# One set of PSUM pools in an attention and soft mixture-of-experts kernel, and another pace in its tail

## The chip, the cores and the metric

The kernel runs on one core of one Trainium2 chip. The time is device microseconds (us) of an execution; a comparison goes by the median of several runs. Engines are called TensorE (PE in the rows), VectorE (DVE), ScalarE (ACT), GpSimd (POOL) and SyncE (SP, whose queue issues all DMAs here). PSUM is the memory that TensorE writes, in 8 banks of 512 fp32 columns by 128 partitions.

## What is computed

Causal attention with a bias from a running sum, on 8 batches of 8 heads, 576 positions of 64 columns; its output, as 4608 tokens of 512 columns, goes through a soft mixture of 8 experts with 4 slots each.

```python
def reference(q, k, v, s, phi, w1, w2):                 # q, k, v (8, 8, 576, 64); s (8, 8, 576)
    scores = q @ k.T / 8                                # per batch and head
    cum = cumsum(maximum(s, 0), -1)
    scores = where(causal, -1e9, scores + minimum(-(cum[:, None] - cum[None, :]), 0))
    attn = exp(scores - max); attn /= attn.sum(-1) + 1e-9
    x = (attn @ v).reshape(4608, 512)                   # tokens
    logits = x @ phi                                    # (4608, 32)
    d = softmax(logits, over tokens); c = softmax(logits, over slots)
    slot_input = (d.T @ x).reshape(8, 4, 512)
    for e in range(8):                                  # w1 (8, 512, 1024), w2 (8, 1024, 512)
        slot_out[e] = maximum(slot_input[e] @ w1[e], 0) @ w2[e]
    return c @ slot_out.reshape(32, 512)                # (4608, 512)
```

## The kernel before

The attention part, up to about 376 us, is a list of operations, each with an engine, an estimated duration, what it comes after, and how many PSUM banks it takes. `schedule` (line 34) puts them in one order per engine; the program is then traced in that order by the loop at line 920. PSUM is divided there into a ring of six banks, `bank()` (line 169, pool `psm`), and two single banks `y` and `sum` (pool `psy`). Where the planner leaves TensorE a gap near the end, `busy(n)` (line 913) fills it with n products of no use. The last operations of the list make the softmax over the tokens final: `m0` to `m7` (lines 794 to 832) end with `i4s`, a scaled 128 x 32 matrix; `t8` (line 780) adds the last batch to `acc`, the sum of tokens by slots; and `ct`/`cd` (lines 706 to 720), per batch, transpose the tokens' weights of the slots and copy them to `ctw`, for the output.

Then `actx.close()` (line 931) releases the list's pools, and the tail follows in the order in which it is written:

- Lines 936 to 945: a new pool `ps4` of eight banks over all of PSUM, given out in turn by `bk()`. The slots' input `sit` is made by four products of `acc` and `i4s`, and copied by VectorE.
- `mlp1` (line 951), the first expert layer, for two groups of four experts: 4 steps of 8 products each with 512 columns, four of them side by side on strips of 32 columns of the array. After each step, `refill` (line 1036) has SyncE load the next four weight blocks of `w2` into the tiles of `w1` that the step was the last to read. `turn` (line 968) transposes the result, with VectorE's copy.
- `mlp2(half, eg)` (line 982), the second layer, for a half of the 512 columns and a group: 8 steps of 4 products of 256 columns. Both groups of a half write one bank, `pso[half]`, in its two halves; VectorE copies the first group's (256 columns), ScalarE the second's.
- `pick(half)` (line 995) sorts the slots by two products `sel`; ScalarE and VectorE make of them `sl[half]`, a high and a low part.
- `result(half, beside)` (line 1010) makes the output: 36 tiles of 128 tokens, two to a bank (`po`), copied by VectorE and ScalarE in turn, and written in nine DMAs of four tiles (512 KB). After every two banks, `result(0)` advances the second layer of half 1 by two steps (line 1029); what is left of it, and `pick(1)`, stand behind its last output. Then `result(1)` runs alone.

All weights are 64 blocks of 512 KB. The first 43 are loaded during the list, into tiles that it does not need or no longer needs; the other 21 are those of `refill`. Every DMA stands in SyncE's one queue, in the order of the text. On this chip an fp32 product is two rows of TensorE in the profile, so a step of `mlp1` is 16 rows and one of `mlp2` is 8.

Of the kernel before, what the change touches and what calls it, by code (L numbers as in the profile page):

```python
# [102 lines left out]
def tile_attn_softmoe(ctx: ExitStack, tc, qk, v, s, phi, w1, w2, cst, out):  # L103
# [9 lines left out]
    NS = 32  # L113
# [20 lines left out]
    tot = top.tile([128, 2], F32, name="tot")  # L134
    nc.vector.memset(tot, 0.0)
    one1 = top.tile([1, 1], F32, name="one1")
    nc.vector.memset(one1, 1.0)
    pre = top.tile([128, NPRE * F], F32, name="pre")

# [23 lines left out]
    one = actx.enter_context(tc.tile_pool(name="one", bufs=1))  # L163
    p2 = actx.enter_context(tc.tile_pool(name="p2", bufs=2))
    pd = actx.enter_context(tc.tile_pool(name="pd", bufs=3, space=bass.MemoryType.DRAM))
    psm = actx.enter_context(tc.tile_pool(name="psm", bufs=6, space=PSUM))
    psy = actx.enter_context(tc.tile_pool(name="psy", bufs=1, space=PSUM))

    def bank(name):
        return psm.tile([128, 512], F32, tag="bank", name=name)  # L170
# [68 lines left out]
    def op(key, eng, ns, prio, fn, after=(), bank=0, frees=None, dma=0, ldw=107, tail=107, mode=0):  # L239

        assert key not in ops, key
        t = prio[0]
        for x in prio[1:]:
            t += PR[x[0]][x[1]] if isinstance(x, tuple) else PR[x]
        ops[key] = dict(eng=eng, ns=ns, prio=round(t, 6), fn=fn, after=[a for a in after if a is not None], bank=bank,
                        frees=frees or [], dma=dma, pt=prio, ldw=ldw, tail=tail, mode=mode)
# [581 lines left out]
    def m7():  # L828
# [2 lines left out]
        nc.vector.reciprocal(t, t)  # L831
        nc.vector.tensor_scalar(i4s, i4, t, st["fac"][:, 1:2], op0=ALU.mult, op1=ALU.mult)

    def load_phi():
        nc.sync.dma_start(out=ph, in_=phi)

# [12 lines left out]
    for i, (e, ns, fn) in enumerate((("PE", 107, m0), ("DVE", 300, m1), ("PE", 60, m2), ("DVE", 100, m3), ("ACT", 220, m4),  # L849
                                     ("DVE", 100, m5), ("PE", 160, m6), ("DVE", 400, m7))):  # L850
        op(("m", i), e, ns, (8.0 * B - 400 + i * 0.1, "soft"), fn, [prev] + {5: [("t4", B - 1)], 6: [("cst",)]}.get(i, []), bank=int(e == "PE"),
           frees=[(("m", i - 1), 0)] if i in (1, 3, 7) else None)
        prev = ("m", i)
    op(("cst",), "SP", 450, (3.0,), (fetch, cst_sb, cst), [("load", 3)], dma=450)
    op(("cw",), "SP", 450, (2.5,), lambda: nc.sync.dma_start(out=cumd, in_=cumhl), [("cum", 1)], dma=800)
    op(("phi",), "SP", 650, (2.0,), load_phi, [("load", 2)], dma=728)
# [56 lines left out]
    def busy(n):  # L913
        d = psy.tile([128, 512], F32, tag="y", name="busy")
        for i in range(n):
            nc.tensor.matmul(d[:, 0:128], ident, ident, start=True, stop=True)
# [16 lines left out]

    tb = ctx.enter_context(tc.tile_pool(name="tb", bufs=1))
    to = ctx.enter_context(tc.tile_pool(name="to", bufs=1))
    ps4 = ctx.enter_context(tc.tile_pool(name="ps4", bufs=8, space=PSUM))

    def bk(name):
        return ps4.tile([128, 512], F32, tag="bk", name=name)

    ps = bk("sit")
    for cc in range(NCC):
        nc.tensor.matmul(ps[:, 32 * cc:32 * cc + 32], acc[:, 128 * cc:128 * cc + 128], i4s, start=True, stop=True)  # L943
    sit = tb.tile([128, NCC, NS], F32, name="sit")
    nc.vector.tensor_copy(sit, ps[:, 0:128].rearrange("p (c s) -> p c s", c=NCC))

    ht = tb.tile([128, 2, NFC, 128], F32, name="ht")

    hs = []

    def mlp1(eg):
        pss = [bk(f"m1{eg}{half}") for half in range(F // 512)]
        for cc in range(NCC):
            for half in range(F // 512):
                for g in range(4):
                    nc.tensor.matmul(pss[half][32 * g:32 * g + 32, :], sit[:, cc, :],  # L956
                                     w1q[4 * eg + g, cc][:, 512 * half:512 * half + 512],
                                     start=(cc == 0), stop=(cc == NCC - 1))
            yield
        relu(eg, pss)  # L960
# [6 lines left out]

    def turn(eg):
        for half in range(F // 512):
            pt = bk(f"ht{eg}{half}")  # L970
            for f in range(4):
                nc.tensor.transpose(pt[:, 128 * f:128 * f + 128],  # L972
                                    hs[eg][:, 512 * half + 128 * f:512 * half + 128 * f + 128], ident)
            nc.vector.tensor_copy(ht[:, eg, 4 * half:4 * half + 4, :], pt.rearrange("p (f x) -> p f x", f=4))
# [2 lines left out]
    cts = [ctw[i // 2][:, 2 * (i % 2):2 * (i % 2) + 2] for i in range((B + 1) // 2)]  # L977

    HC = DM // 2
    pso, sl = [], []  # L980

    def mlp2(half, eg):

        if eg == 0:
            pso.append(bk(f"m2{half}"))
        ps = pso[half][:, HC * eg:HC * eg + HC]
        for fc in range(NFC):
            for g in range(4):
                w = w2q[4 * eg + g, 2 * half + fc // 4]
                nc.tensor.matmul(ps[32 * g:32 * g + 32, :], ht[:, eg, fc, 32 * g:32 * g + 32],  # L990
                                 w[:, HC * (fc % 4):HC * (fc % 4) + HC], start=(fc == 0), stop=(fc == NFC - 1))
            yield
        (nc.scalar.copy if eg else nc.vector.tensor_copy)(sos[half][:, eg, :], ps)  # L993

    def pick(half):

        ps = bk(f"sel{half}")
        for eg in range(2):
            nc.tensor.matmul(ps[0:96, 0:HC], sel[eg], sos[half][:, eg, :], start=(eg == 0), stop=(eg == 1))  # L999
        t = sl[half]  # L1000
        nc.scalar.copy(t, ps[0:96, 0:HC])  # L1001
        nc.vector.tensor_tensor(t[64:96, :], ps[64:96, 0:HC], t[64:96, :].bitcast(F32), op=ALU.subtract)  # L1002
# [3 lines left out]
    def steps(it, n=100):  # L1006
        for _ in range(n):
            next(it, None)

    def result(half, beside=iter(())):  # L1010
        k = 0
        outc = out[:, HC * half:HC * half + HC].rearrange("(t p) c -> p t c", p=128)
        for i in range(0, NO, 4):
            m = min(4, NO - i)
            ot = stage.pop(0)[:, 0:m * HC].rearrange("p (t c) -> p t c", t=m)
            for j in range(0, m, 2):
                n = min(2, m - j)
                po = bk(f"po{half}_{i + j}")[:, 0:n * HC].rearrange("p (t c) -> p t c", t=n)
                for x in range(n):
                    b, c = divmod(i + j + x, 9)  # L1020
                    cv = cts[b].rearrange("p b s -> p (b s)")[:, 128 * c:128 * c + 128]
                    nc.tensor.matmul(po[:, x, :], cv, sl[half], start=True, stop=True)  # L1022
                if k % 2 == 0:
                    nc.vector.tensor_copy(ot[:, j:j + n, :], po)  # L1024
                else:
                    nc.scalar.copy(ot[:, j:j + n, :], po)  # L1026
                k += 1
                if k % 2 == 0:
                    steps(beside, 2)
            nc.sync.dma_start(out=outc[:, i:i + m, :], in_=ot)  # L1030

    again.sort(key=lambda x: x[0])
# [23 lines left out]
    steps(mlp2(0, 0))  # L1056
    steps(mlp2(0, 1))
    pick(0)
    m = chain(mlp2(1, 0), mlp2(1, 1))
    result(0, m)  # L1060
    steps(m)
    pick(1)
    result(1)


# [49 lines left out]
```

## Time and profile before

| | |
|---|---|
| time, median of 3 runs | 443.43 us (442.27 to 443.96) |
| span of the profiled execution | 445.1 us (the page gives no other time of it) |
| TensorE busy | 411.9 us, 93% of the span |
| VectorE, ScalarE, GpSimd busy | 307.0, 245.8, 281.5 us |
| moved by DMA | 83.21 MB, mean 187 GB/s |

The page cuts the span into 40 slices of 11.1 us. In all but the last six TensorE is busy for 0.89 or more of a slice and the DMA engines mostly for 0.3 to 0.7; in the last slices the DMA engines are at 0.8 to 0.99 and move 278 to 414 GB/s, the last two of them with TensorE busy 0.6 and 0. One slice near the tail has a granted TensorE clock of 0.6 to 0.7, where 1 is 2.4 GHz and 0.5 is 1.2 GHz. A profile is one execution; its span stands 1.7 us above the median.

### The profile page before, as it was taken

The page shows a single profiled execution, that of the slowest core. Times are in us where ns is not written, and L with a number is a line of the kernel's source. Part 1 is how long each engine was busy: PE and PEld are TensorE (multiplying, and loading weights), DVE is VectorE, ACT ScalarE, POOL GpSimd, SP SyncE. Part 2 cuts the span into 40 slices and gives each one's busy share as a digit, 9 for nine tenths or more (in the row PEclk, how much of TensorE's full clock was granted, in tenths as well). Part 3 has the DMA queues.
Part 4 walks back from the last instruction along what each step waited for, and adds up shares of the span by engine and source line. Part 5 has one row for each costly group of instructions (what it writes and reads, how often), then busy time and mean ns, then how long its engine had stood idle before and what let it go on. Part 6 is the DMA issues. An engine that isn't in the chain of part 4 may idle for free. (4 is left out here: it accounts for less than half of the span.)

```text
span 445.1 us, 14696 instructions
## 1 busy us (share of the span) xinstructions
PE 411.9 (93%) x5631; PEld 305.1 (69%) x5631; DVE 307.0 (69%) x1055; ACT 245.8 (55%) x732; POOL 281.5 (63%) x385
## 2 busy tenths in 40 slices
PE   8799999989999999999999999999999998998960
PEld 7687777777677767766877677777777766334550
DVE  6777767987887878778877987888685667021460
ACT  2236577576657665856665676576766735021350
POOL 6339989878876896888588868897888700000000
PEclk9699999999999999999999999999999999699995
DMA  5317556636664475447544832461356499899988
GB/s 173 107 46 216 172 161 173 191 107 184 178 194 130 135 207 162 130 134 221 162 127 136 221 87 83 119 185 57 109 135 187 118 300 404 278 414 406 356 279 294
DMA packets 54549, 83.21 MB, mean 187 GB/s; under 512 B 5456, under 2 KB 41808, under 8 KB 54480
## 3 DMA queue, kind: packets, MB, share of 16 engines
q1 hardware_dynamic: 54480, 82.29, 59.0%
q8 instruction: 44, 0.72, 0.7%
q14 instruction: 25, 0.20, 0.1%
HBM read 71.84 MB, written 10.06 MB: 184 GB/s over the span
## 5 line engine op out<-in xcount | busy, mean ns | idle before, releaser
L323 DVE CUSTOM_DVE_ANT_0 junk<-mx,mask 128x448 bf16<-128x448 f32 (+3 forms) x320 | 125.6, 427 | 52.5 <-PE mx L311 27.1
L388 ACT ACTIVATE arena<-s 128x288 f32<-128x288 f32 (+4 forms) x384 | 114.3, 406 | 30.1 <-PE s L377 29.4
L377 PE MATMUL s<-w 64*128 64x288 f32 (+4 forms) x1152 | 109.2, 304 | 0.0
L478 PE MATMUL y<-arena 128*64 128x512 f32 (+4 forms) x640 | 90.1, 427 | 0.0
L377 PEld LDWEIGHTS s<-w 64*128 64x128 f32 (+1 forms) x1152 | 81.9, 177 | 10.0 <-issue 1.2
L395 POOL TENSOR_SCALAR_AFFINE_SELECT arena<-arena 128x256 f32<-128x256 f32 (+1 forms) x160 | 68.1, 437 | 23.3 <-ACT arena L388 21.2
L478 PEld LDWEIGHTS y<-arena 128*64 128x64 f32 x640 | 43.0, 137 | 46.4 <-issue 35.8
L421 POOL TENSOR_TENSOR arena<-arena 128x896 f32<-128x896 f32 x31 | 66.9, 2159 | 7.9 <-PE mt L346 5.9
L311 PE MATMUL mx<-w 64*128 64x288 f32 (+4 forms) x384 | 58.8, 312 | 4.5 <-DVE e_nat L664 2.7
L377 PE MATMUL s<-g 64*128 64x288 f32 (+4 forms) x384 | 56.7, 291 | 0.0
L311 PE MATMUL mx<-g,ones 64*128 64x288 f32 (+4 forms) x384 | 55.1, 305 | 1.3 <-POOL g L217 1.3
L423 POOL TENSOR_TENSOR arena<-arena 128x640 f32<-128x640 f32 x31 | 48.0, 1548 | 2.6
L278 ACT CAST w<-arena 128x576 fp32r<-128x576 f32 x64 | 39.8, 676 | 16.1 <-DMA arena<-in_qk_dram 16.1
L283 DVE TENSOR_TENSOR w<-arena,w 128x576 fp32r<-128x576 f32 x64 | 47.8, 773 | 0.0
L311 PEld LDWEIGHTS mx<-w 64*128 64x128 f32 x384 | 40.6, 189 | 8.7 <-PE s L377 3.9
L490 ACT COPY arena<-y 128x512 f32<-128x512 f32 x32 | 18.8, 588 | 46.6 <-PE y L478 46.6
L311 PEld LDWEIGHTS mx<-g,ones 64*128 64x128 f32 x384 | 40.4, 190 | 2.0 <-POOL g L217 1.5
L540 DVE TENSOR_TENSOR arena<-arena 128x576 f32<-128x576 f32 x31 | 31.6, 1033 | 10.4 <-DMA arena<-rs 10.0
L377 PEld LDWEIGHTS s<-g 64*128 64x128 f32 (+1 forms) x384 | 35.3, 176 | 0.6 <-DMA g<-hl 0.2
L338 POOL TENSOR_SCALAR mh<-mx 128x10 fp32r<-128x10 f32 x32 | 21.1, 658 | 20.6 <-DVE mx L323 20.6
L425 POOL TENSOR_TENSOR arena<-arena 128x384 f32<-128x384 f32 x31 | 31.5, 1015 | 2.4
L323 DVE CUSTOM_DVE_ANT_0 junk<-mx,mask,mx 128x288 bf16<-128x288 f32 x64 | 30.6, 516 | 2.2 <-PE mx L311 1.2
(157 smaller groups left out, 577.0 us busy)
## 6 DMA issues: line engine op xcount, KB each, us to landing
pre<-in_w_dram SPq DMA_DIRECT2D x38, 512.0 KB
arena<-in_qk_dram SPq DMA_DIRECT2D x32, 576.0 KB
arena<-in_w_dram SPq DMA_DIRECT2D x18, 512.0 KB
arena<-rs SPq DMA_DIRECT2D x62, 144.0 KB
arena<-in_v_dram SPq DMA_DIRECT2D x32, 256.0 KB
out_dram<-arena SPq DMA_DIRECT2D x11, 512.0 KB
out_dram<-pre SPq DMA_DIRECT2D x7, 512.0 KB
wg<-in_w_dram SPq DMA_DIRECT2D x5, 512.0 KB
```

The costliest lines, as they stand in the source:

```text
L278: nc.scalar.copy(w[:, QO + S * i:QO + S * (i + 1)], st["raw", p][:, i, :])
L283: nc.vector.tensor_tensor(w[:, QO + S * (2 + i):QO + S * (3 + i)], st["raw", p][:, i, :], w[:, QO + S * i:QO + S * (i + 1)].bitcast(F32), ...
L311: nc.tensor.matmul(ps[a][:, d:d + hi - lo], l[r], t[r, KO + lo:KO + hi], start=t is w, stop=t is gt)
L323: nc.vector.tensor_tensor_reduce(out=junk[r, 0:w], in0=ps[r, d:d + w], in1=mask[r, o:o + w], scale=1.0, scalar=m[:, a, 4:5] if i == 1 else ...
L377: nc.tensor.matmul(ps[a][0:n, d:d + hi - lo], t[r, ko + 128 * j:ko + 128 * j + n], t[r, qo + lo:qo + hi], start=x == 0, stop=x == 3)
L388: nc.scalar.activation(st["p", p][0:n, a, o + lo:o + hi], ps[0:n, d:d + hi - lo], AF.Exp, bias=0.0, scale=0.125)
L395: nc.gpsimd.affine_select(d, d, pattern=[[0, 2], [1, n]], compare_op=ALU.is_ge, fill=0.0, base=0, channel_multiplier=-1)
L421: eng.tensor_tensor(z[:, :, 128:576], pt[:, :, 128:576], pt[:, :, 576:1024], op=ALU.add)
L423: eng.tensor_tensor(z[:, :, 256:576], z[:, :, 256:576], pt[:, :, 1024:1344], op=ALU.add)
L425: eng.tensor_tensor(z[:, :, 384:576], z[:, :, 384:576], pt[:, :, 1344:1536], op=ALU.add)
L478: nc.tensor.matmul(y[r, lo - 64:512], vt[:, j, r], st["p", p][:, g, OFF[j] + lo - 128 * j:OFF[j] + 576 - 128 * j], start=(j == 0), stop=(j ...
L540: nc.vector.tensor_tensor(u, u, st.pop(("r", p)), op=ALU.mult)
```

## The change

There are four edits, all in the tail or next to it.

1. The pools `psm` and `psy` live to the end, and `ps4` is gone: `bk()` becomes `bank()`, six banks in a ring.
2. The slots' input is made by two operations of the list, `sit0` (TensorE, behind three filler products) and `sit1` (VectorE's copy). The last batch's transposes `ct` come after `sit0`. The tile `sit` moves to a pool that lives throughout.
3. `mlp2` writes each group into a bank of its own, `y` and `sum`.
4. `result` takes a list of steps: behind its outputs of four tiles, 2, 3, 3, 3, 3, 3 and 1 steps of what stands beside it, which is the second layer of half 1 and, as its last step, `pick(1)`. The outputs 7 and 8 (counted from 0) have none.

```diff
-    psm = actx.enter_context(tc.tile_pool(name="psm", bufs=6, space=PSUM))
-    psy = actx.enter_context(tc.tile_pool(name="psy", bufs=1, space=PSUM))
+    psm = ctx.enter_context(tc.tile_pool(name="psm", bufs=6, space=PSUM))
+    psy = ctx.enter_context(tc.tile_pool(name="psy", bufs=1, space=PSUM))
...
+    def sit0():
+        busy(3)
+        st["sit"] = bank("sit")
+        for cc in range(NCC):
+            nc.tensor.matmul(st["sit"][:, 32 * cc:32 * cc + 32], acc[:, 128 * cc:128 * cc + 128], i4s, start=True, stop=True)
+
+    def sit1():
+        nc.vector.tensor_copy(sit, st.pop("sit")[:, 0:128].rearrange("p (c s) -> p c s", c=NCC))
...
+    op(("sit", 0), "PE", 900, (8.0 * B - 500, "soft"), sit0, [prev, ("t8", B - 1)], bank=1)
+    op(("sit", 1), "DVE", 290, (8.0 * B - 500, "soft"), sit1, [("sit", 0)], frees=[(("sit", 0), 0)])
+    ops["ct", B - 1]["after"].append(("sit", 0))
...
-    ps4 = ctx.enter_context(tc.tile_pool(name="ps4", bufs=8, space=PSUM))
...
-    ps = bk("sit")
-    for cc in range(NCC):
-        nc.tensor.matmul(ps[:, 32 * cc:32 * cc + 32], acc[:, 128 * cc:128 * cc + 128], i4s, start=True, stop=True)
-    sit = tb.tile([128, NCC, NS], F32, name="sit")
-    nc.vector.tensor_copy(sit, ps[:, 0:128].rearrange("p (c s) -> p c s", c=NCC))
...
-        if eg == 0:
-            pso.append(bk(f"m2{half}"))
-        ps = pso[half][:, HC * eg:HC * eg + HC]
+        ps = psy.tile([128, 512], F32, tag=("y", "sum")[eg], name=f"m2{half}{eg}")[:, 0:HC]
...
-    def result(half, beside=iter(())):
+    def result(half, beside=iter(()), pace=()):
...
-                if k % 2 == 0:
-                    steps(beside, 2)
+            if i // 4 < len(pace):
+                steps(beside, pace[i // 4])
             nc.sync.dma_start(out=outc[:, i:i + m, :], in_=ot)
...
-    m = chain(mlp2(1, 0), mlp2(1, 1))
-    result(0, m)
-    steps(m)
-    pick(1)
+    def rest():
+        yield from chain(mlp2(1, 0), mlp2(1, 1))
+        yield
+        pick(1)
+
+    result(0, rest(), (2, 3, 3, 3, 3, 3, 1))
     result(1)
```

Up to these places every engine has the same instructions in the same order; GpSimd and SyncE have them to the end. The rows below are the built programs' order, without times; a name is the tile written, then the tiles read, and the number in a name only keeps tiles apart.

TensorE at the end of the list, before: filler (`busy`), the last batch's transposes (`ctb`, `cta`), the slots' input (`sit`) and the first product of the first layer (`m`).

```order
L916 MATMUL busy<-ident 128x128 x4
L711 MATMUL ctb_7259<-ident,en_7231 96x128
L711 MATMUL cta_7258<-ident,en_7231 96x128 x4
L943 MATMUL sit<-i4s,acc 128x32 x4
L956 MATMUL m_7289<-pre,sit 32x512 x4
```

The same place now:

```order
L929 MATMUL busy<-ident 128x128 x4
L839 MATMUL sit<-i4s,acc 128x32 x4
L712 MATMUL ctb_7266<-ident,en_7232 96x128
L712 MATMUL cta_7265<-ident,en_7232 96x128 x4
L959 MATMUL m_7285<-pre,sit 32x512 x4
```

The slots' input has moved ahead of the last transposes; there are as many filler products.

TensorE at the first half of the second layer, before: the last transposes of the first layer's result (`ht`), then both groups' products, all on one bank.

```order
L972 MATMUL ht_7402<-ident,h_7393 128x128 x4
L990 MATMUL m_7410<-arena,ht 32x256 x35
L990 MATMUL m_7410<-pre,ht 32x256
L990 MATMUL m_7410<-arena,ht 32x256 x3
L990 MATMUL m_7410<-pre,ht 32x256
```

Now:

```order
L975 MATMUL ht_7398<-ident,h_7389 128x128 x4
L991 MATMUL m_7406<-arena,ht 32x256 x32
L991 MATMUL m_7440<-arena,ht 32x256 x3
L991 MATMUL m_7440<-pre,ht 32x256
L991 MATMUL m_7440<-arena,ht 32x256 x3
```

The products are the same; behind the 32 of the first group the tile written is another one.

TensorE at the end of `result(0)`, before: outputs (`po`, by the number of their first tile), the second layer's products of half 1 (`m`), the pick (`sel`) and the first output of half 1 (`po_0`).

```order
L1022 MATMUL po_24_7586<-sl_7408,ct_6978 128x256 x2
L1022 MATMUL po_26_7590<-sl_7408,ct_6978 128x256 x2
L990 MATMUL m_7490<-pre,ht 32x256 x8
L1022 MATMUL po_28_7603<-sl_7408,ct_6978 128x256 x2
L1022 MATMUL po_30_7607<-sl_7408,ct_6978 128x256 x2
L990 MATMUL m_7490<-pre,ht 32x256 x8
L1022 MATMUL po_32_7620<-sl_7408,ct_6978 128x256 x2
L1022 MATMUL po_34_7624<-sl_7408,ct_6978 128x256 x2
L999 MATMUL sel_7630<-pre,cst_sb 96x256 x2
L1022 MATMUL po_0_7635<-sl_7409,ct_6977 128x256 x2
```

Now:

```order
L1023 MATMUL po_20_7583<-sl_7404,ct_6979 128x256 x2
L1023 MATMUL po_22_7587<-sl_7404,ct_6979 128x256 x2
L991 MATMUL m_7548<-pre,ht 32x256 x8
L1023 MATMUL po_24_7601<-sl_7404,ct_6979 128x256 x2
L1023 MATMUL po_26_7605<-sl_7404,ct_6979 128x256 x2
L1000 MATMUL sel_7609<-pre,cst_sb 96x256 x2
L1023 MATMUL po_28_7615<-sl_7404,ct_6979 128x256 x2
L1023 MATMUL po_30_7619<-sl_7404,ct_6979 128x256 x2
L1023 MATMUL po_32_7624<-sl_7404,ct_6979 128x256 x2
L1023 MATMUL po_34_7628<-sl_7404,ct_6979 128x256 x2
L1023 MATMUL po_0_7633<-sl_7405,ct_6978 128x256 x2
```

The second layer's last products stand two outputs earlier, and the pick stands ahead of the last two outputs of half 0 instead of behind them.

## Rows read from the trace of the kernel before

**Rows 1.** Tail by stretches: length, each engine's busy us, clock, DMA share, GB/s.

```profile
376.00:383.00 7.00, 4.99 (x31) 2.88 (x33) 1.46 (x5) 0.69 (x2) 0.00 (x0) 0.74 1.01 402
...
383.00:386.00 3.00, 3.00 (x20) 0.81 (x16) 0.00 (x0) 0.00 (x0) 0.00 (x0) 0.50 0.32 81
386.00:390.00 4.00, 4.00 (x44) 1.28 (x40) 0.00 (x0) 0.17 (x1) 0.00 (x0) 0.98 0.94 294
390.00:410.00 20.00, 18.47 (x221) 8.26 (x213) 3.52 (x6) 2.96 (x6) 0.00 (x0) 1.00 1.03 412
...
420.00:428.00 8.00, 6.57 (x69) 3.78 (x62) 2.91 (x6) 2.83 (x6) 0.00 (x0) 1.00 0.88 300
428.00:430.00 2.00, 2.00 (x19) 2.00 (x19) 2.00 (x4) 1.87 (x4) 0.00 (x0) 1.00 0.16 57
430.00:443.50 13.50, 1.92 (x17) 1.72 (x15) 3.36 (x6) 2.63 (x6) 0.00 (x0) 0.65 1.02 340
```

**Rows 2.** The same view, two stretches, for the clock (third number from the end).

```profile
378.00:380.00 2.00, 1.22 (x9) 1.18 (x8) 0.00 (x0) 0.69 (x2) 0.00 (x0) 0.84 1.04 416
...
408.00:410.00 2.00, 1.09 (x5) 0.47 (x4) 0.42 (x1) 0.51 (x2) 0.00 (x0) 1.00 1.05 410
```

**Rows 3.** SyncE in order of time: start, length, what it issues, how many.

```profile
384.39 9.42 SPq L838 DMA_DIRECT2D pre<-in_w_dram  x12
...
411.16 7.04 SPq L1030 DMA_DIRECT2D out_dram<-arena  x5
```

**Rows 4.** TensorE's waits from 376 to 446, all: us, times, longest.

```profile
PE po L1022 <- DVE sl L1002: 1.8, 2, 0.9
PE m L990 <- DVE pre L993: 1.4, 2, 0.9
PE sit L943 <- ACT ct L720: 0.8, 1, 0.8
PE ctb L711 <- DVE en L704: 0.7, 1, 0.7
PE sel L999 <- ACT pre L993: 0.5, 1, 0.5
PE m L956 <- issue: 0.5, 1, 0.5
```

**Rows 5.** TensorE, then VectorE, in order of time at the end of the list.

```profile
375.51 1.06 PE L916 MATMUL busy<-ident 128*128 128x128 f32 x8
...
377.44 0.60 PE L711 MATMUL cta<-ident,en 128*96 128x128 f32 x4
378.82 1.47 PE L943 MATMUL sit<-i4s,acc 128*128 128x32 f32 x8 [0.78 <-ACT ct L720]
...
375.92 0.30 DVE L832 TENSOR_SCALAR i4s<-cst_sb,tot,fac 128x32 f32<-128x32 f32 x1
...
380.38 0.29 DVE L945 COPY sit<-sit 128x128 f32<-128x128 f32 x1 [3.21 <-PE sit L943]
```

**Rows 6.** The chain that ended last, in the tail: start, length, what, rows merged.

```profile
380.77 13.16 PE m L956 x96
...
394.96 3.62 PE m L956 x32
...
404.04 3.66 PE m L990 x64
...
409.78 0.74 PE po L1022 x4
410.51 1.00 PE m L990 x16
411.52 0.67 PE po L1022 x4
...
427.35 2.92 PE po L1022 x22
...
432.77 0.60 DVE pre L1024
```

More of the change, by code (lines that the diff above doesn't have):

```diff
@@ L136, in tile_attn_softmoe @@
     one1 = top.tile([1, 1], F32, name="one1")
+    sit = top.tile([128, DM // 128, NS], F32, name="sit")
     nc.vector.memset(one1, 1.0)
@@ L935, in tile_attn_softmoe @@
     to = ctx.enter_context(tc.tile_pool(name="to", bufs=1))
-    ps4 = ctx.enter_context(tc.tile_pool(name="ps4", bufs=8, space=PSUM))
-    def bk(name):
-        return ps4.tile([128, 512], F32, tag="bk", name=name)
-    ps = bk("sit")
-    for cc in range(NCC):
-        nc.tensor.matmul(ps[:, 32 * cc:32 * cc + 32], acc[:, 128 * cc:128 * cc + 128], i4s, start=True, stop=True)
-    sit = tb.tile([128, NCC, NS], F32, name="sit")
-    nc.vector.tensor_copy(sit, ps[:, 0:128].rearrange("p (c s) -> p c s", c=NCC))
     ht = tb.tile([128, 2, NFC, 128], F32, name="ht")
@@ L951, in mlp1 @@
     def mlp1(eg):
-        pss = [bk(f"m1{eg}{half}") for half in range(F // 512)]
+        pss = [bank(f"m1{eg}{half}") for half in range(F // 512)]
         for cc in range(NCC):
@@ L969, in turn @@
         for half in range(F // 512):
-            pt = bk(f"ht{eg}{half}")
+            pt = bank(f"ht{eg}{half}")
             for f in range(4):
@@ L979, in tile_attn_softmoe @@
     HC = DM // 2
-    pso, sl = [], []
+    sl = []
     def mlp2(half, eg):
-        if eg == 0:
-            pso.append(bk(f"m2{half}"))
-        ps = pso[half][:, HC * eg:HC * eg + HC]
+        ps = psy.tile([128, 512], F32, tag=("y", "sum")[eg], name=f"m2{half}{eg}")[:, 0:HC]
         for fc in range(NFC):
@@ L995, in pick @@
     def pick(half):
-        ps = bk(f"sel{half}")
+        ps = bank(f"sel{half}")
         for eg in range(2):
@@ L1017, in result @@
                 n = min(2, m - j)
-                po = bk(f"po{half}_{i + j}")[:, 0:n * HC].rearrange("p (t c) -> p t c", t=n)
+                po = bank(f"po{half}_{i + j}")[:, 0:n * HC].rearrange("p (t c) -> p t c", t=n)
                 for x in range(n):
```

## The prediction, made before the changed kernel was run

> **What bounds the kernel now.** I read the page first (the span, the slices, the chain), then the last 70 us by stretches [rows 1], then what SyncE issues [rows 3] and what TensorE waits for [rows 4], and last the chain through the tail [rows 6]. The order of instructions shows that up to 375 us each engine does what it did before, so only the tail can move the time. There the reader is to see two things.
>
> First, the DMA engines bound the tail, not TensorE. From 376 on they have to bring the last of the first 43 weight blocks, then 21 more into tiles that the first layer has finished with, and to write 18 outputs, 512 KB (0.524 MB) each. Their share is about full at 412 GB/s while they read and at 340 while they write [rows 1], and after TensorE's last product (it starts its last run of them at 427.35) they write for 13 us more [rows 1, 6]. The span ends 1.6 us behind the last write.
>
> Second, they run dry twice. From 383 to 390 they carry 81 and then 294 GB/s, because SyncE issues nothing until 384.39 [rows 1, 3]: the first block of the 21 goes into a tile that the first layer must have read. From 420 to 430 they carry 300 and then 57, because outputs come too slowly and then, around the second pick, not at all [rows 1]. What the change is worth is what it fills of these two holes; a TensorE that is early by more than that gains nothing.
>
> **The holes in us.** By bytes the first is (412 - 81) x 3 / 412 + (412 - 294) x 4 / 412 = 2.4 + 1.1 = 3.5; by the DMA share (1 - 0.32) x 3 + (1 - 0.94) x 4 = 2.3. The second is by bytes, against the 340 of pure writing, (340 - 300) x 8 / 340 + (340 - 57) x 2 / 340 = 0.9 + 1.7 = 2.6; by share 1.0 + 1.7 = 2.7. Together 5.0 to 6.1 us [rows 1]. That is the ceiling of the gain, whatever TensorE does: the same bytes are moved at the same rates.
>
> **Part 1: the input of the slots, made in the list.** Before, its products stood behind the last transposes and waited 0.8 us for ScalarE's copy of these, since the new pool takes over the banks of the old [rows 4]; they ran from 378.82 for 1.47 us, VectorE's copy and the hops took until 380.77 [rows 5, 6]. Now they stand ahead of the last transposes. Their input i4s is there at 375.92 + 0.30 = 376.2, TensorE's filler ends at 375.51 + 1.06 = 376.6 [rows 5] (there are four filler products as before: one from the list, three in the new step), so they run from 376.6 to at most 378.1. The transposes behind them took about 0.7 us (from 377.32, the first one, to 378.04 [rows 5]); the copy (0.29 [rows 5]) lies beside them. The first layer starts at 378.8 instead of 380.77: **2.0 us earlier**. The transposes end some 0.7 us later than before; their ScalarE copies feed only outputs 30 us on, so that costs nothing.
>
> The clock is the other half of it. The granted clock falls between 378 and 380, mean 0.84 (from 2.4 to 1.2 GHz), is 0.50 from 383 to 386 and back at 0.98 from 386 on [rows 1, 2], after TensorE had stood still 0.7 us for the transposes' input, 0.8 for ScalarE's copy and 0.5 for the slots' input [rows 4]. For the first layer 96 matmul rows take 13.16 us where 32 take 3.62, that is 13.16 - 3 x 3.62 = **2.3 us** lost [rows 6]. The change fills the first two of these stops and hides the third under the transposes, so I take the clock to stay up: 2.3 us more. If it falls again, that is a rival.
>
> The first reloads wait for the first 16 matmul rows of that layer, 3.62 / 2 = 1.8 us, and are issued from 380.6 on, while the earlier loads still run (402 GB/s until 383). So **hole one closes**, and reading goes on at 412.
>
> **Part 2: a bank per group.** In both halves of the second layer the second group's matmuls waited for the copy of the first group, since both wrote one bank: 1.4 us in two waits [rows 4]. Now they write different banks. In the first half that is 0.5 us on the chain; the second half's 0.9 is inside the output steps.
>
> **Part 3: the pace.** First product of an output: 409.78 - 2.0 - 2.3 - 0.5 = 405.0. An output of four tiles takes 0.67 us, two steps of the second layer 1.00 [rows 6]. Group 0 thus lasts 1.67, groups 1 to 5 with three steps 0.67 + 1.5 = 2.17 each, so group 6 begins at 405.0 + 1.67 + 10.85 = 417.5 and the pick follows at 418.2 instead of behind group 8. The pick's own chain (about 1.6 us) now runs beside groups 7 and 8 (1.34 us), and half 1 begins at about 420 where it began at 427.35 [rows 6]: **7.4 us earlier on TensorE**.
>
> **What is late next.** The old flow is full until 383, and of the 81 x 3 = 243 KB after it about half is still its own: it ran out at about 383.2. With no hole, the 21 reloads, 11.0 MB at 412, take 26.7 us and end at 409.9; each output then adds 0.524 MB / 340 = 1.54 us. An output is issued 1.4 us after its first product (411.16 against 409.78 [rows 3, 6]) and flows about 0.8 later. Group 6 is the tightest: it can flow at 417.5 + 1.4 + 0.8 = 419.7, and the writes ahead of it end at 409.9 + 6 x 1.54 = 419.1, so some 0.6 us of a hole stays. Groups 7, 8 and half 1 come faster than 1.54 us each. So 18 outputs end at 409.9 + 27.7 + 0.6 = 438.2, and the span at 439.8.
>
> **The sum.** The ceiling of 5.0 to 6.1 less the 0.6 that stays is 4.4 to 5.5; the step-by-step working gives 445.1 - 439.8 = 5.3. I take 5.2, near the second since it rests on bytes. The profiled execution's span is 445.1, 1.7 above the median of 443.43; the gain is subtracted from the median: **438.2 us**, own range 437.0 to 439.3. The 7.4 us of TensorE are not the gain: some 2 us of them end as writes still draining with every engine done.
>
> **Banks.** The ring of outputs has six banks now where it had eight with the second layer's in it. VectorE's and ScalarE's copies set the pace of half 1 as before (427.35 to 433.37 [rows 6], 6 us for 9 outputs), well under 9 x 1.54 of writing; at nothing, therefore. If copies blocked TensorE there for 1 us, the writes would still cover it.
>
> **Rivals.** (a) **The clock falls all the same** under the first layer. Then 2.3 us of TensorE are not won: the first reload comes at about 382.4, hole one keeps some 0.8, and group 6 comes 2.3 - 0.8 later, so the gain is 5.2 - 0.8 - 1.5 = 2.9: 440.5. For it: the slots' products are mostly weight loading (in 378 to 380 that was busy 1.18 us of the 1.22 [rows 2]), and I move them, not remove them. Against: between 408 and 410 TensorE was busy 1.09 of 2 us and the clock stayed at 1.00 [rows 2].
>
> (b) **The last weights come late.** The steps of the second layer stand earlier, and if a weight is missing, TensorE waits with the outputs queued behind it, and VectorE, ScalarE and SyncE's writes wait for these. Before, TensorE waited for no DMA in the tail (all six of its waits are in [rows 4]). The last four blocks are needed in group 4, at about 405.0 + 1.67 + 3 x 2.17 + 0.67 + 0.5 = 414.4. If loads drain ahead of outputs they are there by about 412 (409.9 and some 2 of landing, an estimate from the 1.6 between the first reload's issue and the flow's return at 386 [rows 1, 3]); if the three outputs issued by then share the engines, by 412 + 3 x 1.54 = 416.6, a wait of 2.2 us, of which hole two gets all: gain 5.2 - 2.2 = 3.0, 440.4. No row decides between the two. The Trainium skill, DMA: Bandwidth & Descriptors, section Queues, rings and completion order, says that each engine takes the descriptors of one ring in their order; by that the loads go first and the wait is zero.
>
> (c) **The DMA does not gain from being fed earlier**: reads and writes overlap for longer, and in overlap the flow is below the sum I made. Or the change leaves the holes elsewhere. Bound: the gain vanishes, 443.
>
> (d) **Slower: the clock falls and stays down** through the second layer and the outputs. From 378.8 to 405.0 it has 4 x 3.62 + 2 x 3.66 = 21.8 us of matmuls at the full clock [rows 6]. Each us that passes at 1.2 GHz loses half a us, so the gain of 5.2 is gone after about 10 us of it, and past 15 us the kernel is slower by over 0.5%; all of it low is 438.2 + 21.8 = 460. In the trace the low stretch goes from about 379.4 (0.84 over 2 us is 0.64 us at half) to 386.2, 6.8 us, and stops while the first layer runs densely [rows 1, 2]. The Trainium skill, TensorE: Matmul & The Clock Gate, section A second HAM failure mode: psum-queue depth-cycling, speaks against this change: short stops between groups that cycle through banks made the clock swing there. By that rule the paced stretch, with fewer banks, would be the place. The trace disagrees so far: its paced stretch shows 1.00 from 408 to 410 and from 420 to 430 [rows 1, 2].
>
> **Chances.** Forecast 0.62; (a) 0.14; (b) 0.12; (c) 0.09; (d) 0.03. The bound of 0.5%, about what a measurement of this kernel tells from no change, is 2.2 us: faster is below 441.2. Forecast, (a) and (b) lie there but for a little of the two last (0.02): faster 0.86, same 0.11, slower 0.03. The range of 8 in 10 takes in forecast, (a) and (b), 0.88 in all, and the ceiling of 6.1 with the scatter of the runs (443.43 less 442.27, 1.2) below: 436.2 to 441.0.
>
> **What would show it.** Right: the first layer starts at about 379 at a clock of 1.00; SyncE's first reload is issued near 380.6 and no stretch from 376 on falls under 0.9 of DMA share until the last write; the first output product near 405, the second pick near 418; TensorE waits in the tail for no second-layer copy. Wrong: a clock of 0.50 after 379 (a), TensorE waiting for a weight load near group 4 (b), full DMA share at fewer than 340 GB/s (c), a clock of 0.50 after 405 (d). A hole near 419 larger than 0.6 would say that the pace, not the bytes, sets the end.

## The result, and the profile after

| | before | changed |
|---|---|---|
| median, us (lowest to highest of 4) | 443.69 (442.27 to 444.85) | 438.27 (436.97 to 439.66) |
| ratio, 95% interval | | 0.9879 (0.9846 to 0.9911) |
| profiled execution: span, us | 445.1 | 437.9 |

The changed kernel is 1.2% faster: 5.4 us by the medians, where 5.2 were forecast, and 438.27 us where 438.2 were. That it came within 0.1 us is luck: the same kernel gave 440.69 in the repeat below. The profiled execution's own time was 439.66 at a span of 437.9, so this one lies 1.4 above its median; with the same 1.8 between span and time, that of before lay about 3.2 above its own.

The tail after, by stretches: length, each engine's busy us, clock, DMA share, GB/s. It answers to [rows 1].

```profile
376.00:378.00 2.00, 2.00 (x23) 1.82 (x25) 1.17 (x4) 0.00 (x0) 0.00 (x0) 1.00 1.03 412
378.00:380.00 2.00, 2.00 (x20) 0.58 (x24) 0.00 (x0) 0.69 (x2) 0.00 (x0) 1.00 1.02 408
380.00:383.00 3.00, 3.00 (x32) 0.91 (x28) 0.00 (x0) 0.00 (x0) 0.00 (x0) 1.00 0.98 352
383.00:386.00 3.00, 3.00 (x32) 0.91 (x28) 0.00 (x0) 1.20 (x2) 0.00 (x0) 1.00 0.98 333
386.00:390.00 4.00, 4.00 (x40) 1.67 (x36) 0.91 (x2) 0.00 (x0) 0.00 (x0) 1.00 1.02 387
390.00:410.00 20.00, 19.02 (x249) 9.94 (x240) 4.77 (x9) 3.70 (x7) 0.00 (x0) 1.00 1.02 406
410.00:414.00 4.00, 4.00 (x56) 2.31 (x56) 1.63 (x3) 1.18 (x2) 0.00 (x0) 1.00 1.09 385
414.00:419.00 5.00, 5.00 (x45) 3.92 (x43) 3.06 (x6) 3.44 (x7) 0.00 (x0) 1.00 1.04 365
419.00:419.50 0.50, 0.50 (x4) 0.34 (x4) 0.50 (x2) 0.50 (x2) 0.00 (x0) 1.00 0.72 252
419.50:424.00 4.50, 4.20 (x26) 3.14 (x24) 4.50 (x9) 3.80 (x8) 0.00 (x0) 1.00 1.03 353
424.00:436.00 12.00, 0.00 (x0) 0.00 (x0) 0.41 (x1) 0.32 (x1) 0.00 (x0) 0.52 1.04 345
```

Read the share, second from the end: both holes of [rows 1] are gone but for half a microsecond at 0.72; but from 380 to 390 the rate, the last number, is under 412 at a full share. Then the clock, third from the end: it stays at 1.00 where it had been 0.50 from 383 to 386. The last row shows what is left as the bound: 12 us of writing at full share with TensorE idle.

All of TensorE's waits from 370 to 440 after (us, times, longest), which answer to [rows 4]. Of the six there, five are gone, and the outputs wait for a pick once, not twice (the second row lies ahead of 376).

```profile
PE po L1023 <- DVE sl L1003: 0.9, 1, 0.9
PE pn L808 <- DVE mrow L804: 0.3, 1, 0.3
```

The chain that ended last after, in the tail (start, length, what, rows merged), which answers to [rows 6].

```profile
377.98 10.44 PE m L959 x96
...
403.50 0.73 PE po L1023 x4
...
405.91 1.43 PE m L991 x24
...
414.97 2.78 DMA out_dram<-arena
...
418.50 3.39 DMA out_dram<-pre
```

The 96 matmul rows take 10.44 us, not 13.16, and from 415 on the chain goes through the writes.

### The profile page after: what moved, and what is told of

The parts are those of the page before. It is cut to its first block, busy times and chain, and to the rows that moved or that the text cites. A ratio compares the mean times of both kernels' runs of the same rounds, so it can differ in the third digit from the quotient of the medians.

```text
span 437.9 us, 14693 instructions
## 1 busy us (share of the span) xinstructions
PE 408.1 (93%) x5631; PEld 304.5 (70%) x5631; DVE 306.5 (70%) x1055; ACT 246.4 (56%) x732; POOL 282.5 (65%) x385
## 4 chain that ended last, share of the span: by engine, by line
PE 71%; DMA 10%; DVE 9%; issue 3%; POOL 2%; SPq 2%; ACT 1%; DVEq 0%
PE s L378 21%; PE y L479 16%; PE mx L312 11%; DMA arena<-rs 5%; PE m L959 3%; PE m L991 3%; PE sum L508 3%; DMA rs<-sr 2%; DVE nmin L736 2%; PE busy L929 2%; PE nat L549 2%; PE lt L620 2%; DVE arena L541 2%; SPq L518 1%; PE sl L774 1%
```

## The experiments

The times of single runs of one kernel differ by up to 7 us (29 runs of the kernel before: 439.44 to 446.43), more than the parts of this change are worth. In the traces most of the scatter lies ahead of the tail: `i4s` on VectorE, the last operand of the slots' input, ends at 375.92 in one execution of the changed kernel and at 377.60 in another, and from 373.45 to 377.60 over all of the traces. Behind it the two executions of the changed kernel have TensorE's first layer and first output at the same distances to 0.01 us (the two of before differ by 1.3 at the first output, as the clock stayed low for longer in one). So I judge parts by the tail, counted from the end of `i4s`, one trace for each kernel, and look whether the medians agree. For the smaller parts they cannot say: on the chip where the whole change gave 440.69, taking away the pace, the move or the bank gave 439.15, 439.38 and 440.71, with intervals that overlap. The medians in the table come from four sets on different chips, in which the kernel before had 443.69 (the two rows of the result), 444.09 (changed again, pace back, slots' input back, one bank), 443.47 (before again, pools alone, no filler, three writes less) and 443.85 (the others).

In the table, worked out from each trace, the times in us count from the end of `i4s`. Holes are the sum of (1 - DMA share) over those whole stretches of half a microsecond, from `i4s` to the last write, in which the share is under 1. "Reads left" are the bytes read from the end of `i4s` on, and "to move at 22" all bytes, read or written, that are still to move 22 us later, both in MB.

| kernel | first layer | first output product | first of half 1 | last write ends | holes | reads left | to move at 22 | median, us |
|---|---|---|---|---|---|---|---|---|
| before | 4.55 | 33.56 | 51.13 | 67.49 | 5.3 | 13.97 | 15.81 | 443.69 |
| before, again | 4.17 | 32.22 | 49.78 | 66.08 | 5.5 | 13.30 | 15.62 | 444.54 |
| pools alone | 3.02 | 29.37 | 46.93 | 63.28 | 2.7 | 13.45 | 14.69 | 442.14 |
| pools and slots' input | 1.98 | 28.34 | 45.91 | 62.25 | 1.9 | 13.75 | 14.21 | 441.35 |
| changed, one bank | 1.98 | 28.34 | 43.55 | 62.30 | 1.9 | 13.22 | 14.23 | 440.71 |
| changed, slots' input back | 3.02 | 28.62 | 42.88 | 61.85 | 2.1 | 12.93 | 14.82 | 439.38 |
| changed, pace back | 1.98 | 27.58 | 44.18 | 60.56 | 0.8 | 13.90 | 14.35 | 439.15 |
| changed | 1.98 | 27.58 | 41.84 | 60.64 | 0.75 | 13.30 | 14.26 | 438.27 |
| changed, again | 1.98 | 27.58 | 42.00 | 61.01 | 1.6 | 12.83 | 14.33 | 440.69 |
| changed, no filler | 1.75 | 27.35 | 41.61 | 60.46 | 0.2 | 13.81 | 14.25 | 439.00 |
| the same, again | 1.75 | 27.35 | 41.61 | 60.40 | 0.6 | 13.20 | 14.09 | 438.88 |
| changed, full rows last | 1.76 | 27.36 | 46.27 | 62.12 | 2.8 | 13.29 | 14.23 | 439.49 |
| changed, three writes less | 1.98 | 27.57 | 41.84 | 56.47 | 1.0 | 13.54 | 12.65 | 435.36 |

Take the holes from the end of the last write: in the eleven traces of experiments and of the changed kernel with all writes, 59.3 to 60.6 us are left, whatever TensorE did. That of before has 62.2. With the same lists it had 0.67 MB more of its reads still to do at `i4s` than the changed one (13.97 against 13.30 MB), which at 412 GB/s is 1.6 us.

The reads left differ by up to 1.1 MB from one execution to the next, and with them the holes ahead of 22 us, so holes are best compared between traces with like reads left. What is still to move at 22 us does not follow them: in the eight traces with the slots' input in the list and all writes it is 14.1 to 14.35 MB, whatever was left at `i4s`. It tells what the first hole cost. The 22 us from `i4s` on, of before again, pools alone, pools and slots' input, changed, and pace back (22 times the last number is what they moved):

```profile
374.50:396.50 22.00, 19.91 (x160) 8.27 (x159) 2.88 (x7) 3.08 (x6) 0.00 (x0) 0.92 0.88 324
376.26:398.26 22.00, 20.80 (x209) 8.84 (x211) 3.91 (x8) 3.08 (x6) 0.00 (x0) 1.00 0.98 373
373.88:395.88 22.00, 21.94 (x227) 9.42 (x226) 3.92 (x8) 3.08 (x6) 0.00 (x0) 1.00 1.02 408
375.92:397.92 22.00, 21.93 (x231) 9.69 (x234) 3.92 (x9) 3.08 (x6) 0.00 (x0) 1.00 1.01 385
373.45:395.45 22.00, 21.94 (x231) 9.66 (x234) 3.92 (x8) 3.08 (x6) 0.00 (x0) 1.00 1.03 409
```

**Both kernels again.**

> The kernel before once more, for a second trace of it. Theory: from the end of i4s the first layer starts 4.5 us later with the clock at 0.50 under it, and there are two holes in the DMA share, near 8 and near 52 us after i4s, 5 us in all. Rival (the clock fell only in the one execution shown): clock at 1.00, the first layer about 2.3 us shorter, the first hole under 1.5 us.

> The changed kernel once more, as the base of the other runs. Theory (the DMA engines set the end; the change filled their two holes): 5.2 us under before, full DMA share from 376 to the last write. A rival (it was only that one execution whose loads were early in the list): under 3 us.

Measured against the kernel before on the same chip: before again 1.0032 (0.9994 to 1.0069), changed again 0.9908 (0.9874 to 0.9941), 440.69 us. The second interval covers most of the first result's, so 0.985 to 0.994 is what can be said of the ratio. The repeat of before had 13.30 MB left at `i4s`, as the changed kernel had; its last write ends at 66.08 against 60.64. So of the 7.2 us between the two first spans, 5.4 are the change, and 4.7 of these are holes. By the medians of its chip the repeat of the changed kernel is 3.4 us faster, where 5.2 were expected and the rival said under 3.

The repeat of before by stretches (columns as above). The hole and the fall of the clock are in both profiled executions of before. Not every execution has the fall, though: of the 29 runs of before on one chip, the four with a mean granted clock of 0.982 took 439.44 to 440.95 us and the nine with 0.968 to 0.972 took 444.61 to 446.08. At 0.982 TensorE is at 1.2 GHz for about 16 us in all; the shortest such stretches in any trace here are 6.8 us at the start and, in the traces of before, 8.5 at the end, which by this estimate leaves no room for a fall of 3.4 in the tail. So part of the scatter of before is this fall.

```profile
378.00:380.00 2.00, 1.51 (x10) 0.53 (x13) 0.29 (x1) 0.00 (x0) 0.00 (x0) 0.73 0.88 336
380.00:382.00 2.00, 2.00 (x16) 0.74 (x12) 0.00 (x0) 0.00 (x0) 0.00 (x0) 0.50 0.24 96
382.00:385.00 3.00, 3.00 (x32) 1.03 (x27) 0.00 (x0) 0.00 (x0) 0.00 (x0) 0.94 0.62 158
...
424.00:427.00 3.00, 2.72 (x22) 2.72 (x23) 2.40 (x5) 1.94 (x5) 0.00 (x0) 1.00 0.44 157
```

The repeat of the changed kernel had only 12.83 MB of reads left, ran out sooner and shows a small rest of hole one:

```profile
381.00:382.00 1.00, 1.00 (x16) 0.28 (x12) 0.00 (x0) 0.00 (x0) 0.00 (x0) 1.00 0.96 393
382.00:383.00 1.00, 1.00 (x12) 0.26 (x8) 0.00 (x0) 0.00 (x0) 0.00 (x0) 1.00 0.71 193
383.00:384.00 1.00, 1.00 (x16) 0.36 (x12) 0.00 (x0) 0.00 (x0) 0.00 (x0) 1.00 0.83 279
```

**Do the writes set the end?** The last three writes of half 1 are left out, with everything on the engines kept:

```diff
-            nc.sync.dma_start(out=outc[:, i:i + m, :], in_=ot)
+            if half == 0 or i < 24:
+                nc.sync.dma_start(out=outc[:, i:i + m, :], in_=ot)
```

> The changed kernel without the last three of its 18 writes: output tiles 24 to 35 of half 1 are made and copied but stay unwritten. Theory (writes set the end): 3 x 1.54 = 4.6 us less than the changed kernel. Rival (TensorE and the copies set the end, the writes follow at their heels): under 1.5 us less, the latency of the last write apart.

Measured: 435.36 us, 0.9793 (0.9748 to 0.9837), the last write at 56.47 instead of 60.64, 4.2 us earlier. The last stretches of this kernel:

```profile
420.00:432.00 12.00, 3.42 (x20) 2.43 (x18) 4.14 (x7) 3.45 (x7) 0.00 (x0) 0.69 1.00 336
432.00:433.50 1.50, 0.00 (x0) 0.00 (x0) 0.00 (x0) 0.00 (x0) 0.00 (x0) 0.50 0.00 1
```

The share is full to about 431.5 and the end follows it. Three writes are worth 3 x 1.54 = 4.6 by the rate; nearly all of that comes off. By the medians it is 3.6 under the kernel without filler on the same chip. So the transfers set the end, no engine does.

**The pools alone.** Slots' input behind the list, without the three filler products that the list has in front of it; one bank for both groups, old pace (the diffs of these two stand below); only the pools live throughout.

```diff
-    op(("sit", 0), "PE", 900, (8.0 * B - 500, "soft"), sit0, [prev, ("t8", B - 1)], bank=1)
-    op(("sit", 1), "DVE", 290, (8.0 * B - 500, "soft"), sit1, [("sit", 0)], frees=[(("sit", 0), 0)])
-    ops["ct", B - 1]["after"].append(("sit", 0))
...
     actx.close()
+    sit0()
+    sit1()
```

> The changed kernel with everything undone but the pools: slots' input behind the list, both groups in one bank, old pace. So what is left of the change is that nothing waits for a new pool. Theory (that wait of 0.8 us is what lets the clock fall): first layer 3.0 us after i4s at clock 1.00, half 1 about 46.5 us after i4s instead of 51.1 before and 41.8 with the whole change, holes of about 3 us instead of 5.3: 2.5 to 3 us under before. Rival (moving the slots' input is what counts): clock at 0.50 under the first layer, holes of 4.5 to 5, within 1 us of before.

Measured: 442.14 us, 0.9960 (0.9927 to 0.9992), 1.3 to 2.4 us under the medians of before on that chip; holes 2.7 instead of 5.5. TensorE in order of time at the end of the list, first in the repeat of before, then here (start, length, line, what, count, idle before and what ended it):

```profile
375.60 0.28 PE L711 MATMUL ctb<-ident,en 128*96 128x128 f32 x1 [0.75 <-DVE en L704]
375.72 0.60 PE L711 MATMUL cta<-ident,en 128*96 128x128 f32 x4
377.10 1.08 PE L943 MATMUL sit<-i4s,acc 128*128 128x32 f32 x8 [0.78 <-ACT ct L720]
378.67 5.77 PE L956 MATMUL m<-pre,sit 128*32 128x512 f32 x36 [0.49 <-issue]
```

```profile
377.36 0.29 PE L712 MATMUL ctb<-ident,en 128*96 128x128 f32 x1 [0.75 <-DVE en L705]
377.48 0.60 PE L712 MATMUL cta<-ident,en 128*96 128x128 f32 x4
377.92 0.98 PE L838 MATMUL sit<-i4s,acc 128*128 128x32 f32 x8
379.28 4.93 PE L956 MATMUL m<-pre,sit 128*32 128x512 f32 x44 [0.38 <-DVE sit L841]
```

The stop of 0.78 us for ScalarE's copy is gone, the other two stand, and the clock stays up, at a share of the DMA that is nearly full:

```profile
378.00:380.00 2.00, 1.62 (x17) 1.07 (x19) 0.29 (x1) 0.69 (x2) 0.00 (x0) 1.00 1.02 406
380.00:382.00 2.00, 2.00 (x24) 0.64 (x20) 0.00 (x0) 0.00 (x0) 0.00 (x0) 1.00 0.91 356
...
424.00:425.00 1.00, 1.00 (x11) 1.00 (x10) 1.00 (x3) 1.00 (x3) 0.00 (x0) 1.00 0.11 38
425.00:426.00 1.00, 1.00 (x11) 1.00 (x10) 1.00 (x3) 1.00 (x4) 0.00 (x0) 1.00 0.49 171
```

So the clock stays up without the move of the slots' input, here and in the kernel with the slots' input back, and falls in both traces of before: the pools' edit is enough for it as far as two traces on either side can show. What is to move at 22 us goes from 15.62 to 14.69 MB by the pools, 2.3 us at 412 GB/s, out of 1.36 MB or 3.3 us by the whole change. The larger part of the first hole is the pools'; the second remains.

**The slots' input, added and taken away.** First the pools and the list's input, with one bank (its diff stands below) and the old pace; then the whole change without the move (and without the filler products in front of it), whose diff is that of the kernel with the pools alone.

```diff
-            if i // 4 < len(pace):
-                steps(beside, pace[i // 4])
+                if k % 2 == 0:
+                    steps(beside, 2)
```

> The changed kernel with one bank for both groups and the old pace: pools and slots' input only. Of the two, undoing the pace alone had left the holes at 0.5 us and undoing the banks alone at 1.8. Theory (outputs at the old, shorter groups are queued early enough, so the wait between groups is what costs): half 1 about 45.6 us after i4s, holes of 1 to 2 us, tail 1 us longer than with the whole change, 4 under before. Rival (the two edits are worth nothing each, but one of them is needed): holes of over 2.5 us.

> The changed kernel with the slots' input made behind the list, after the last transposes, from the same banks (so without the wait for ScalarE's copy). Theory: the first layer starts 1.8 us later at a high clock, and since group 6 has no margin nearly all of it shows: 1.5 to 1.8 us slower than the changed kernel; if the clock falls too, 3.5 to 4. Rival (writes cover a late TensorE): under 0.5, only a short hole near 383.

Measured: 441.35 us, 0.9932 (0.9897 to 0.9968), 2.5 us under before by the medians where 4 were expected; and 439.38, 0.9886 (0.983 to 0.9942). The move is worth 3.02 - 1.98 = 1.04 us on TensorE in both pairs. The holes differ by 0.8 and 1.35, but at unlike reads left; against the repeat of the changed kernel, with 12.83 MB left beside 12.93, it is 0.5. At 22 us the move has brought 14.69 - 14.21 = 0.48 and 14.82 - 14.26 = 0.56 MB, 1.2 to 1.4 us. Taking it away was expected to cost 1.5 to 1.8 us; the last write is 0.85 to 1.2 later than in the two traces of the changed kernel, and the median does not show it. Without it the clock stays at 1.00 too, but the first reload is late for the DMA:

```profile
381.00:383.00 2.00, 2.00 (x26) 0.53 (x18) 0.00 (x0) 0.00 (x0) 0.00 (x0) 1.00 0.53 166
```

**The bank.** Both groups of a half in one bank again, in the changed kernel:

```diff
+        if eg == 0:
+            pso.append(psy.tile([128, 512], F32, tag=("y", "sum")[half], name=f"m2{half}"))
-        ps = psy.tile([128, 512], F32, tag=("y", "sum")[eg], name=f"m2{half}{eg}")[:, 0:HC]
+        ps = pso[half][:, HC * eg:HC * eg + HC]
```

> The changed kernel with both groups of a half in one bank again. Theory: TensorE waits 0.5 us between the groups of half 0 and about 0.9 between those of half 1, group 6 comes 1.4 later, and 1.0 to 1.4 us show. Rival (the writes queued cover it): under 0.3.

Measured: 440.71 us, 0.9932 (0.9899 to 0.9965). Its wait, and three of its stretches:

```profile
PE m L993 <- DVE pre L996: 1.4, 2, 0.9
```

```profile
414.00:415.00 1.00, 1.00 (x16) 0.58 (x8) 0.00 (x1) 0.00 (x0) 0.00 (x0) 1.00 0.64 215
...
416.00:417.00 1.00, 1.00 (x10) 0.82 (x7) 0.33 (x1) 0.47 (x2) 0.00 (x0) 1.00 0.58 200
...
419.00:421.00 2.00, 2.00 (x17) 1.84 (x16) 2.00 (x4) 1.78 (x4) 0.00 (x0) 1.00 0.84 292
```

The wait of [rows 4] is back to the tenth. It costs 1.7 us of TensorE up to half 1 and 1.15 of holes, all of it later than 22 us. At the old pace it is the same: the holes later than 22 us are 1.8 with one bank (pools and slots' input) and 0.6 with two (pace back). The median, 440.71 against 440.69 for the whole change on that chip, does not show it. The outputs come with so little ahead of the DMA that a wait of that size there shows.

**The pace.** Two steps behind every output, and the pick behind the last, in the changed kernel:

```diff
-            if i // 4 < len(pace):
-                steps(beside, pace[i // 4])
+                if k % 2 == 0:
+                    steps(beside, 2)
...
-    result(0, rest(), (2, 3, 3, 3, 3, 3, 1))
+    m = chain(mlp2(1, 0), mlp2(1, 1))
+    result(0, m)
+    steps(m)
+    pick(1)
```

> The changed kernel with the old pace: two steps after each two banks, the second pick behind the last output of half 0. Theory: TensorE comes to half 1 at about 421 instead of 418; the writes queued by then end at about 422 to 423, and half 1's first output flows at about 423: a hole of 0.3 to 1.6 us before half 1, so about 1 us slower than the changed kernel, 4.2 under before. Rival (the pace is what filled the second hole, 2.6 us): 2.6 slower than the changed kernel. Rival (the pace is hidden): no difference.

Measured: 439.15 us, 0.9924 (0.9881 to 0.9967); the last write at 60.56 against 60.64, holes 0.8 against 0.75. Half 1 comes 2.3 us later on TensorE and the DMA does not feel it:

```profile
417.00:419.00 2.00, 1.37 (x8) 1.37 (x9) 1.23 (x3) 0.67 (x2) 0.00 (x0) 0.79 1.07 379
419.00:420.00 1.00, 1.00 (x7) 1.00 (x6) 0.84 (x2) 0.63 (x2) 0.00 (x0) 0.50 0.62 220
420.00:422.00 2.00, 2.00 (x13) 2.00 (x13) 1.68 (x3) 1.35 (x3) 0.00 (x0) 0.60 1.02 355
```

At the old pace a group of half 0 comes every 0.67 + 1.00 = 1.67 us, not every 2.10, so more writes are queued when the pick comes, and the later half 1 costs a hole of 0.4. The new pace has its own small one at 419. Later than 22 us the holes are 0.6 at the old pace against 0.3 in the changed kernel, and with one bank 1.8 against 1.5: the pace saves 0.3 us of holes, which neither the last write nor the median (439.15 against 440.69 for the whole change on that chip) shows. With one bank the old pace has one hole around the pick; this is the stretch in the kernel with pools and slots' input:

```profile
420.00:422.00 2.00, 2.00 (x14) 2.00 (x14) 1.67 (x3) 1.17 (x3) 0.00 (x0) 0.70 0.28 96
```

**The filler.** The step of the list that makes the slots' input begins with three filler products; these are taken out.

```diff
     def sit0():
-        busy(3)
         st["sit"] = bank("sit")
```

> The changed kernel without the three filler products ahead of the slots' input, so that TensorE stands still some 0.7 us there. Theory: one stop of that length does not bring the clock down, so no difference in time. Rival (the filler holds the clock): 0.50 under the first layer, that layer 2.3 us longer, tail 2 to 3 us longer.

> The changed kernel without the filler once more, as the base of the version with full rows, on the same chip: 4.5 to 5 us under before, holes of 0.3 us.

Measured: 439.00 us, 0.9886 (0.9842 to 0.9931), and 438.88, 0.9898 (0.9851 to 0.9945). TensorE now stops ahead of the slots' input:

```profile
PE sit L838 <- DVE i4s L833: 0.5, 1, 0.5
```

```profile
384.00:386.00 2.00, 2.00 (x26) 0.52 (x16) 0.00 (x0) 0.00 (x0) 0.00 (x0) 1.00 1.03 410
```

The second execution, with 13.20 MB of reads left and not 13.81, reads more slowly there at a full share:

```profile
380.00:383.00 3.00, 3.00 (x36) 0.91 (x32) 0.00 (x0) 0.00 (x0) 0.00 (x0) 1.00 1.02 340
```

The clock stays at 1.00 without the filler in both, and everything behind it is 0.23 us earlier, since the last filler product ends after `i4s` is there. By the medians this is no different from the changed kernel.

**Full rows for the last outputs.** To win more, the bytes must move at a higher rate. Here the last twelve tiles are written in whole rows of 512 columns, twice the length, once both halves are there; no filler.

```diff
-    result(0, rest(), (2, 3, 3, 3, 3, 3, 1))
-    result(1)
+    result(0, rest(), (3, 3, 3, 3, 6), end=24)
+    rows(24)
+    result(1, end=24)
```

> A version meant to beat both: the changed kernel without the filler, second layer of half 1 within groups 0 to 4, the pick ahead of group 5; then the tiles 24 to 35 are written in full rows of 512 columns (six writes of 2 KB a row and tile in place of twelve half ones), and half 1 of the tiles 0 to 23 behind them. Theory (writes set the end, and a write of 1 KB pieces runs at 340 GB/s where reads of 4 KB pieces run at 412): the six writes gain up to 0.25 us each, 1.5 us less than without, if TensorE is not late to them. Rival (the piece's size is not what slows writes): no difference.

Measured: 439.49 us, 0.9906 (0.987 to 0.9942): no gain.

```profile
414.00:416.50 2.50, 2.17 (x18) 1.97 (x17) 1.87 (x4) 1.72 (x4) 0.00 (x0) 1.00 0.27 94
...
420.00:424.00 4.00, 2.35 (x15) 1.65 (x13) 2.92 (x5) 2.48 (x5) 0.00 (x0) 1.00 1.03 380
...
428.00:432.00 4.00, 0.00 (x0) 0.00 (x0) 0.00 (x0) 0.00 (x0) 0.00 (x0) 0.50 1.03 338
```

The whole rows do flow faster, at 380 GB/s against 338 for half rows. But all of the writes together take 26.9 us of the engines instead of 27.5, and with both halves needed sooner, five outputs and not seven stand ahead of the second pick: a hole of 2.1 us at 414 takes more than is won.

## Why the prediction was right, point by point

**The bound and the ceiling: right.** The forecast rested on the DMA, not on TensorE's 7.4 us. Measured, half 1 comes 51.13 - 41.84 = 9.3 us earlier on TensorE and the last write 5.4 (against the repeat of before). Taking writes away moved the end; taking the pace away did not. The rival (c), that earlier feeding gains nothing, is out, though its sign showed: a full share under 340 GB/s, 333 from 383 to 386.

**The holes by share or by bytes: by bytes, though the profiled execution hides it.** I took 5.2, near the sum by bytes, on the claim that reading goes on at 412 once hole one is closed. In this execution it did not: 352, 333 and 387 GB/s from 380 to 390 at a full share. Against 412 that is 60 x 3 + 79 x 3 + 25 x 4 = 517 KB or 1.25 us. But it had less to read at `i4s` than that of before. The three traces of experiments with 13.75 to 13.90 MB left, about as much as before had, read at 401 to 412 from 6 to 10 us after `i4s`; the one with 13.54 at 363 to 389; the five with the slots' input in the list and 12.83 to 13.30 at 291 to 346, at shares of 0.94 to 1.02. So the slow reading goes with the reads left, not with the change; why it does is open. Between pace back (13.90 MB left) and before (13.97) the bytes to move at 22 us differ by 15.81 - 14.35 = 1.46 MB, which is 3.5 us at 412: the first hole by bytes, not the 2.3 by share. By share, the holes that closed are 4.6 to 4.8 (3.7 to 3.9 in the repeat); the last write came 5.4 (5.1) earlier than in the repeat of before, and the difference lies in the rate.

**Part 1: the sum about right, the reason wrong.** The first layer starts 2.6 us earlier from `i4s` (2.0 forecast), and the clock gives 13.16 - 10.44 = 2.7 (2.3 forecast); against the repeat of before, where it was low for 3.4 us and not 6.8, the two are 2.2 and 1.7. But I gave all of it to the moved products. The pools alone bring 1.15 to 1.5 of the start and all of the clock; on top of them the move brings 1.04. The move without the pools was not run. The step that failed is "the change fills the first two of these stops and hides the third": one stop less was enough in both traces that have it. Whether filling one of the other two would also have been enough was not tried. Rival (a) is out.

**Part 2: right, and worth more than its place in the sum.** Forecast 0.5 on the chain and 0.9 inside the output steps; measured 28.34 - 27.58 = 0.76 and 43.55 - 41.84 - 0.76 = 0.95 on TensorE, 1.1 us of holes.

**Part 3: the times right, the credit wrong.** First output product 403.50 (405.0 forecast), first product of half 1 at 417.76 (about 420), a rest of a hole at 419 of about 0.15 us (0.6 forecast). Of the 2.2 us between 420 and 417.76, 1.5 are the earlier start and 0.5 a slip in my sum: the second layer of half 1 has 16 steps, so group 5 has two left and not three, and lasts 1.67 us and not 2.17. But the second hole was closed by what came before: TensorE is 4.6 to 6 us earlier at the first output, and the bank takes the wait out. The pace by itself is worth 0.3 us of holes and nothing in the last write. My step "half 1 7.4 us earlier" counted as if the old pace, started some 5 us earlier, would still have run dry; at 1.67 us a group it queues writes ahead and has the same margin.

**Rivals (b) and (d).** TensorE waits for no load in the tail, so the last weights were not late. The clock is 1.00 from 376 to 424, in the paced stretch too, so (d) is out. TensorE had hardly a stop in that stretch (busy 4.00 of 4.00 us from 410 to 414, 5.00 of 5.00 from 414 to 419). The psum-queue depth-cycling that the Trainium skill, TensorE: Matmul & The Clock Gate, section A second HAM failure mode: psum-queue depth-cycling, tells of did not appear there with a ring of six banks; without the stops that it speaks of, this stretch does not test it. At the old pace the clock did dip, to 0.50 at 419, behind the waits for the second pick, and the last write came no later.

**The banks at nothing: right.** TensorE waits for no output bank.

## What to carry to other kernels

Add up the holes in the bound resource first, by busy share and by bytes: that is the ceiling, and a faster engine beyond it is only earlier at the same end. A new PSUM pool opened in the middle of this kernel put a wait of 0.78 us, for the last copy from the old banks, in front of its first product; look for such a wait before filling the stop behind it with filler. And when several edits feed one hole, take each away alone as well as adding it alone, since whichever closes it first gets the gain.

## What the runs showed of the hardware

Three stops of TensorE close together (0.75, 0.78 and 0.49 us) were followed by a fall of its clock from 2.4 to 1.2 GHz in both profiled executions of before, for 6.8 and 3.4 us. Two stops (0.75 and 0.38) were not, in two kernels, and neither was one of 0.47, in three traces. Stops alone do not settle it: one of 1.8 to 2.5 us, which ends between 365.5 and 368.1 us, stands in eight of the traces; the clock fell for 3.4 us during it or within 1.5 us of its end in three of them (1.93, 2.18 and 2.20) and not in the other five (1.84, 1.88, 2.10, 2.33 and 2.45).

A write in pieces of 512 columns moved 380 GB/s, in pieces of 256 columns 338 to 353. Reads moved 406 to 412 at a full share in most stretches; from 6 to 10 us after `i4s`, in five traces that had 12.83 to 13.30 MB of reads left there, they moved 291 to 346 at shares of 0.94 to 1.02: a full share does not say that bytes move at the full rate.

A kernel on a single core scattered by 7 us over 29 runs, and its time went with the mean granted clock: 439.4 to 441.0 us at 0.982, 444.6 to 446.1 at 0.972 and less.
